# Sliding-window attention and a gated convolution block: w_in in three parts, shifted V in halves, batch 0's masks by matmul, a new order

## The chip, the cores and the metric

The kernel runs on one core of a Trainium2 chip. Its time is the device time of one execution in microseconds; the figure of comparison is the median over several executions. A profile is one execution, and has a span of its own (first to last instruction). The engines are PE (TensorE), DVE (VectorE), ACT (ScalarE), POOL (GpSimd) and SP (SyncE, which here only issues DMAs); each runs its own instructions in order and waits on semaphores for the others.

## The reference

Eight batches of 576 tokens with 8 heads of 64. The first half is attention inside a window of 32 tokens to each side; the second is a feed-forward block whose hidden layer is gated by a convolution of three taps along the sequence.

```python
scores = scale * q @ k.T                      # per batch and head
scores = where(|i - j| <= 32, scores, -1e9)
x = softmax(scores) @ v                       # -> (8, 576, 512)
h = max(x @ w_in, 0)                          # w_in (512, 1024)
conv[t] = sum_k conv_w[k] * h[t + k - 1]      # zero outside the sequence
out = (h * sigmoid(conv)) @ w_out             # w_out (1024, 512)
```

All inputs and the output are float32; the kernel computes in bfloat16 with float32 sums.

## The kernel before

**Attention.** For a batch `b` and a group `i` of four heads, `load_qk` brings q and k into a staging tile `st`, `cast_qk` turns them to bfloat16 (`qkb`), `transposes` turns them by TensorE into `qkT` (an `ev` copy of PSUM follows for each half), and `scores` makes, for 64 queries at a time, the products with the 128 keys around them. Those 128 keys are one window's reach, so that every score tile is 128 keys by 64 queries with the same band inside; `exp` (ACT) writes them to `attn`, and `mask` multiplies the result by a band of ones and zeros (DVE or POOL). No maximum is subtracted. `values` (`av`) multiplies V by it. V carries a 65th column of ones, so the sum of weights comes with the product; `rec` and `mul` divide by it.

**Plain and shifted V.** Query tiles begin every 64 tokens, so every second one needs the V rows from the middle of one 128-row block to the middle of the next. `load_v` and `cast_v` fill `ve`, with the plain blocks; `shift_v` makes `vo`, whose upper half is the lower half of `ve`'s block (`vo hi`) and whose lower half is the upper half of the next block (`vo lo`). For batches 0 and 1 this is done block by block; for the others four blocks at a time, in one operation for each half. The order says on which engine: a copy by DVE or POOL, or a DMA from SBUF to SBUF. Before, 11 of the 12 operations of batches 2 to 7 are DMAs of 260 KB, issued by SP.

**Feed-forward.** Two batches make three chunks of 384 tokens (`c` from 0 to 11); `unit` handles 128 hidden features of a chunk (`m` from 0 to 7): `ph` (four matmuls of x, turned, and `w_in`), `relu`, the three taps, `tanh`, `gate`. A tap is a matmul with a diagonal weight block (`diag_w`, built by `diag m`, three instructions), a DVE operation, or a POOL product (`cp`, and `cs` for the sum of two). The table `CONV` has a letter for each unit: 3, 2 and 1 for the number of taps on TensorE (the rest on DVE), q, r and s for kinds with POOL. Then `project` (`py`) multiplies by `w_out`, `y` copies the result and `store` writes it. `turn` brings the attention's output to x turned, by TensorE (`xt`, `ex`) or by a DMA transpose (`xd`), as `TURNS` says.

**What sets the order.** Nothing is scheduled at run time. Every operation has a number, and the string `ORDER` (lines 102 to 191) names each with its engine's letter (P, V, S, G, D for SP's DMAs) and its buffers; `Work.emit` walks it. What an engine does is thus fixed in order: what waits holds everything behind it on that engine, and for SP this means every later DMA. `F` in the order stands for filler matmuls on zeros. `load_w` brings w_in and w_out through slots of the same `st` ring in halves of 1 MB, and `cast_w` turns each 128-column block to bfloat16. Helper `InOrder` (line 232) issues every instruction, so all have that line in the profile.

POOL's order up to the last cast of batch 1's k, by names: cast v 0 0, diag 1, cast q 0 0, diag 2, 0, 5, 6, cast q 0 1, diag 7, 3, 4, two vo copies of batch 0, cast w_in 1, 0, one vo copy, cast w_in 6, 4, cast q 1 0, cast k 1 0, one vo copy, cast q 1 1, cast k 1 1.

Of the kernel before, what the change touches and what calls it, by code (L numbers as in the profile page):

```python
# [10 lines left out]
BF16 = mybir.dt.bfloat16  # L11
# [29 lines left out]
class Work:  # L41
# [44 lines left out]
BUFS = {'st': 3, 'qkb': 5, 'qkT': 3, 'attn': 2, 'rec': 4, 'xn': 3, 'hT0': 8, 'hT1': 6, 'hT2': 6, 'cp': 2, 'gT': 4, 'y': 7}  # L86
TURNS = ('eeeee', 'eeede', 'eeeed', 'dedde', 'ddddd', 'ddddd', 'ddddd', 'edddd')
CONV = (
    '33333333',
    '33q3323r23223321',  # L90
    's222r32q',
    '1232s332',
    '22q22q22',
    'q31s2qrq',
    '33212q2s',
    'r2rq312q',
    'qq23q1q2',
    'r3rqrq23',
    '12qrrq1q',
    '2rrr2rrq',  # L100
)
ORDER = """
15D 11D0 12D 1F 17D 2F 13D1 2F 14D 7F 28G 0V 1P0 2F 2V 33V 1F 4G 4F 20G0 21S 2F 16D 5G 1F 22S1 41P120 42P 23S 3G
45P34 44V 1F 43S 1F 46P 8G 2F 48S 47V 1F 9G 1F 30S 2F 49P5600 24G2 25S 54P214 2F 37V 18D 55S 1F 10G 1F 51S 1F 120D2
59P321 60P 52S 26V3 1F 27S 1F 6G 62V 1F 63P60 19D 61S 1F 64P 1F 36V 50S 121D0 1F 7G 65V 2F 130D1 66S 2F 53V 29S 1F
67P2351 1F 57S 56S 1F 35G 131D 72P604 70S 1F 31V 68S 2F 34G 1F 73S 2F 38V 74S 1F 39V 1F 58V 69S 3F 75S 123G 135D 1F
125S 77P10 86P5 124S 71V 95P2 3F 122G 78V0 96V1 1F 87V2 79S 2F 32V 132D2 2F 76V 97S 3F 40G 88V 1F 133D 98P6 89P0
113P3 99V3 107P4 90V0 104P1 100V 80P2 128G 129S 1F 114V1 105V2 1F 81V3 91V 102P5 127S 126G 106V 1F 93P6 82S 108V0
103V 139G4 109V 115S 84P7 94V 111P0 231D0 85S 112V 118P1 156P522 140G0 119V 134D 241P4 158S 157V 285P3 242S00 263P6
286S1 144V 243P7 264S2 149G 287P0 261S 150V 265P1 141G1 305S 262V 307P2 283S 306V 159P54 284V 142G2 308S3 172P360  # L110
161V 329P7 136D 174S 160V 173S 309P0 351P1 330S4 327S 331P2 232D1 352S5 328V 162P4650 233G 234S 353P3 349S 235V 137D
373P7 165S 164S 350V 163S 175P10 374V6 143G 167P526 371S 395P4 176V 236S 985D 170S 166V 375P7 169S 517P1 396S7 145G
372V 473P6 168S 177V 397P2 152G 393S 429P4 415S 171V 178P3501 138D 430S01 238S 239G 518V1 583P4 416V 181S 519P1 240S
237G 474V2 539P0 986D 394V 180S 451P2 482G0 983D2 561P6 179S 148V 495P7 481G1 584S3 188P51 151V 452S4 417P3 483G
496V5 537S 987D 189V2 190S 981D0 538V 146G 453P4 982D 183P271 182V 562S1 984D 471S 197P5 147S 418P 595G0 186S 198V3
484V6 185S 155G 199V 431P1 184S 472V 497P7 153V 421P5 419S0 154V 994V 988D 515S 187V 540S4 206P4 449S 422P 493S
992S3 450V 207V0 494V 516V 209P2 596V3 200P0 208S 191P1 218P6 996G 210V1 201V2 215P7 192V3 211V 202S 193V 542P2
219V1 213P4 216V0 423V1 195P1 217S 989D 204P0 220V 224P5 196V 990S4 425P6 991G0 225V3 543V 226V 1076D1 1017P711 214S
205V 221D 229P5 559S 426P 1077D 230S 993G1 1018V 1001P402 560V 1080D 427S2 1019V 1004P57 1078D0 627P2 1003S 1002V
1079D 605P6 1006S 715P1 997G 628V0 649P0 606S1 1005V 716S2 629P4 608P7 998G 717P2 647S 650V3 671P6 597V 735S 693P1  # L120
648V 1085G2 672S4 652P5 736V 603S 1020P04 609V 694S5 674P6 604V 625S 695P2 1022V 1021S 737P1 759P3 713S 626V 738S7
563P0 675V 760S6 793P4 714V 581S 1082D 995V 691S 1007P7130 582V 1086S3 1000D 692V 740P2 653V 764P0 815P6 741V 1008S
794V02 1010S 816V2 757S 837P7 809G1 1009S 765V 808G0 758V 1012P436 669S 838S5 766V 781P1 1087G4 670V 1014S 1015S
1081D 1013S 1096P270 1011V 779S 782P 1097S 810G 780V 1098V 1099P53 783S3 1083D 1023P6421 1016V 811P0 1100S 999D
840P7 424D 1088G0 812V 1024S 818P1 859P5 1084D 1101V 1026S 813S 420D 1025S 1112P622 1089G 841V 784D 881P3 860S4 428D
814V 1027G 1113S 1735D2 1114V 862P4 882S3 785P5 857S 819V 863V 1028P062 1737D1 1092S 1033P32 858V 1736D 835S 786P
1738D 1034V2 879S 893G1 836V 1029S 1051P7 1035V 1090G 1031S 1042P1 880V 787S4 1060P0 903P3 1091G 1052V1 1030S 1061V0
1043V3 1053V 925P2 1094D 894V4 904S1 1741D 947P5 1062V 926S0 895V 905P6 1044V 948S5 1115P73 1032V 901S 928P0 923S
955G0 1117V 789P2 1116S 1744G1 924V 1036P1 929V 1045P5 1069P3 1063P7 1054P6 1037V2 956G1 790P 1046V1 945S 1064V0
1038V 1065S 1746G2 1055V3 1047V 1070V2 1040P1 1056V 1049P5 791S5 1071V 1067P7 957G 1058P6 1050S 902V 1072D 1755P321  # L130
1068S 946V 973P4 1745G3 1059S 1756V 1041S 1740D 1102P5070 1757V 1747S4 969P6 788D 958V3 1739D 1093V 1171P1 1105S
1103S 1095D 1104S 1193P2 1172V03 967S 1106G 1215P7 1742D 1750S 1194V2 1107P501 968V 1216S1 1832D0 1176P2 1110S
1196P3 1108S 1177V 970P 1109S 1197V 1833Q 1118P7151 1743D 1178V 1749G 1213S 1237P0 1073D 1120S 1111V 1830D2 974P
1121S 1831D 1191S 1748G 1214V 1238S5 792D 1192V 1128P10 1119S 1146P5 975V6 1155P3 1137P0 971S1 1259P2 1122G 1147V1
1129V0 1156V3 1138V2 1148V 1123P746 1139S 1130V 1217P5 1260V4 1125S 1240P1 1157V 1126S 1277P0 1124S 1303P2 1241V
1835D 1235S 1274G1 1325P4 1257S 1127V 1842S0 1281P3 1275G0 1236V 1158P6 1140P7 1304V7 1326S3 1751G 1131P5 1282S6
1258V 1149P4 1752G 1164P2 1150V1 1305P3 1159V0 1165V2 1151S 1834D 1141V3 1276G 1160V 1283P1 1166V 1323S 1132V0 972D
1328P6 1142V 1754G 1301S 977P2 1278V 1302V 1279S 1144P4 1324V 1771P710 1145S 1280V 978P 1836D 1840G1 1772S 1329V
976D 1161D 1133V 1774P34 1345S 1773V 1758P07 1753D 1839G2 979S0 1347P5 1134D 1759S 1346V 980D 1776V 1844S 1841G4
1169P1 1850P262 1838D 1170S 1348P 1760V 1775S 1843G 1851V 1761P0410 1349S3 1852V 1351P7 1762S 1350D 1845G 1763S  # L140
1766P325 1764S 1853P60 1767S 1765V 1866P411 1352P 1769S 1768S 1868V 1854S 1770G 1837D 1777P3521 1867V 1353S2 1355P1
1855V 1778S 1152D 1780S 1782P647 1354D 1779S 1356P 2491D1 1785S 1784S 2492D 1783S 1781V 2489D2 1359P3 1357S4 1786V
1787P01 2490D 1360S00 1805P2 1814P5 1358D 1796P7 1806V2 1381P4 1788V1 1815V3 1807S 1797V0 1847V 1798V 1403P6 1816S
1382V1 1362P1 1846V 1384P3 1404S2 1789V 1447P7 1363V 1412G0 2495D 1385V 1425P2 1379S 1411G1 1448S3 1817P4 1380V
1401S 1413G 1790P5 1450P0 1426S4 1818V0 1791V2 1402V 1823P6 1808P7 2500G3 1428P1 1451V 1469P2 1809V3 1824V1 1467S
1429V 1810S 1799P3 1468V 1825V 1445S 1491P0 1800V3 1414V7 1826D 1470S5 2501S2 1547P6 1446V 1477G0 1801V 1513P2
2498G1 1492V0 1423S 1869P13 1792V 1548S21 1424V 1494P0 1514S1 1793D 1478G1 1569P5 1870V 1871S 2494D 1479G 2499S4
1827D 1516P6 1819V 1535P7 1495V 1820D 1555G1 1517V 1570S4 1591P2 1511S 1480V3 1533S 1613P1 1512V 1556G0 1489S 2493D
1534V 1592S1 1571P4 1802D 2504G 1614V3 1848D 1635P5 1589S 1557G 1490V 1849D 1596P0 1856P6210 1590V 1636S0 1536P
1597V 1628G0 1857S 1558V3 1859S 1858S 2496D 1861P456 2503G 1598V 1567S 1631P1 1811D 1539P2 1862S 1860V 1611S 1629G1  # L150
1568V 1701P4 1864S 1863S 1612V 1630G 1540P 1537S5 1702V5 2502S 1538D 1872P6351 1865V 1541S1 1877P074 2497D 1874S
1709G1 1632V 1657P2 2584D0 1879S 1710G0 1542D 1679P3 1878S 2586D1 1711G 1875S 1882P72 1873S 2587D 1891P0 1900P5
1883V1 1880S 1892V3 1633S 1909P6 1884V 1638P4 1658S4 1881V 1543P7 2585Q 2505G 1893V 1680S2 1910V2 1925P2 1634V 1911S
1665G0 2589D 1901V0 1639V 2507D 1544P 1926S22 1902V 1655S 1876V 1927P0 1545S6 1947P3 1712V1 2506S 1546D 1656V 1918P6
1945S 1691G1 1894P2 1885P5 1948S0 1919V1 1903P7 1946V 1912P4 1721S 1991P3 1895V3 1913V2 1904V0 1896S 1920V 2508D
2593G0 1914V 2035P0 1886V1 1905S 1722V 2509P640 1887V 1921D 1969P2 1992S1 1692V1 2510S 2594G1 2511V 1949P5 1970S5
2013P7 1693V 2036S6 1888D 1666G1 1967S 1727P3 2014V7 1699S 1667G 1968V 2016P6 1700V 2079P4 1922D 2592Q 2043G1 2017V
# [36 lines left out]
def kernel(  # L194
# [67 lines left out]
    diag_w = sb.tile([128, 3, MB, 128], BF16, name="diag_w")  # L262
    ident = sb.tile([128, 128], BF16, name="ident")
    ident24 = sb.tile([3 * MB, 3 * MB], FP32, name="ident24")
    mask = sb.tile([128, 18, 64], BF16, name="mask")
    zero = sb.tile([128, 512], BF16, name="zero")


# [541 lines left out]
```

The softmax here doesn't subtract the row's maximum and nothing guards it: scores larger than these inputs give would overflow.

## Time and profile before

| | us |
|---|---|
| median of 13 executions (lowest, highest) | 228.05 (225.87, 230.52) |
| the profiled execution: time, span | 230.52, 228.8 |
| first feed-forward matmul (`pf<-xT,w_in_sb`) | 25.48 |
| busy: PE, DVE, ACT, POOL | 212.1, 197.7, 187.4, 140.0 |
| half clock granted in the attention and feed-forward work, near | 90 to 94 |
| DMA moved in all | 48.16 MB |

A line of a group or a time line names the engine, the operation, the tile written and those read, with shapes, and in brackets the idle time before it and what ended it. The clock row has a digit for each fortieth of the span (5.72 us), in tenths of full speed, and 9 is full. Matmuls overlap, so the mean duration of one is longer than the time from start to start.

### The profile page before, as it was taken

The page shows a single profiled execution, that of the slowest core. Times are in us where ns is not written, and L with a number is a line of the kernel's source. Part 1 is how long each engine was busy: PE and PEld are TensorE (multiplying, and loading weights), DVE is VectorE, ACT ScalarE, POOL GpSimd, SP SyncE. Part 2 cuts the span into 40 slices and gives each one's busy share as a digit, 9 for nine tenths or more (in the row PEclk, how much of TensorE's full clock was granted, in tenths as well). Part 3 has the DMA queues.
Part 4 walks back from the last instruction along what each step waited for, and adds up shares of the span by engine and source line. Part 5 has one row for each costly group of instructions (what it writes and reads, how often), then busy time and mean ns, then how long its engine had stood idle before and what let it go on. Part 6 is the DMA issues. An engine that isn't in the chain of part 4 may idle for free.

```text
span 228.8 us, 7189 instructions
## 1 busy us (share of the span) xinstructions
PE 212.1 (93%) x2720; PEld 123.1 (54%) x2720; DVE 197.7 (86%) x467; ACT 187.4 (82%) x474; POOL 140.0 (61%) x203
## 2 busy tenths in 40 slices
PE   7698899989989995999999988999999999999993
PEld 5367558558455642555555545545555565455441
DVE  6289779899999985698899868998999999899990
ACT  2699899998989694789989979779979899777642
POOL 5988656653575855784268945865475745476540
PEclk9799999999999998899999999999999999999999
DMA  6999999999989999999994999995606311501224
GB/s 194 342 290 376 360 263 252 340 295 287 256 227 328 246 144 293 315 241 201 279 314 99 185 263 370 180 204 155 186 14 133 105 46 37 183 1 49 92 93 182
DMA packets 66390, 48.16 MB, mean 211 GB/s; under 512 B 50780, under 2 KB 50804, under 8 KB 66356
## 3 DMA queue, kind: packets, MB, share of 16 engines
q1 hardware_dynamic: 64992, 46.32, 77.2%
q10 hardware_dynamic: 1364, 1.39, 3.4%
q8 instruction: 21, 0.34, 0.8%
q14 instruction: 13, 0.11, 0.2%
HBM read 32.52 MB, written 9.44 MB: 183 GB/s over the span
## 4 chain that ended last, share of the span: by engine, by line
PE 52%; ACT 14%; DMA 13%; DVE 13%; issue 4%; POOL 2%; SPq 1%; DVEq 0%; POOLq 0%; ACTq 0%
PE pf L232 52%; DMA vst<-in_v_dram 10%; ACT attn L232 5%; DVE gT L232 3%; DMA st<-in_k_dram 3%; DVE pf L232 3%; DVE qkT L232 2%; ACT pf L232 2%; ACT xn L232 1%; ACT qkb L232 1%; DVE attn L232 1%; DVE xn L232 1%; ACT y L232 1%; DVE hT L232 1%; DMA xT<-xn 1%
## 5 line engine op out<-in xcount | busy, mean ns | idle before, releaser
L232 PE MATMUL pf<-xT,w_in_sb 128*128 128x385 bf16 (+2 forms) x416 | 74.0, 317 | 3.2 <-ACT hT L232 0.7
L232 PE MATMUL pf<-w_out_sb,gT 128*128 128x512 bf16 x288 | 72.2, 380 | 0.0
L232 POOL TENSOR_SCALAR cp<-hT,conv_w_sb 128x384 f32<-128x384 bf16 (+1 forms) x63 | 40.3, 645 | 47.5 <-ACT hT L232 20.0
L232 ACT ACTIVATE pf<-pf 128x384 f32<-128x384 f32 (+1 forms) x104 | 48.4, 479 | 12.3 <-DVE pf L232 10.2
L232 DVE SCALAR_TENSOR_TENSOR gT<-pf,hT 128x384 bf16<-128x384 f32 (+1 forms) x104 | 52.1, 517 | 5.4 <-ACT pf L232 4.9
L232 PEld LDWEIGHTS <-w_in_sb 128*128 128x128 bf16 x416 | 38.8, 98 | 27.2 <-issue 3.6
L232 ACT ACTIVATE attn<-pf 128x512 bf16<-128x512 f32 (+1 forms) x96 | 41.4, 523 | 2.4 <-PE pf L232 2.4
L232 ACT ACTIVATE hT<-pf 128x385 bf16<-128x385 f32 (+2 forms) x76 | 35.6, 490 | 6.0 <-PE pf L232 5.7
L232 PEld LDWEIGHTS <-gT 128*128 128x128 bf16 x288 | 26.0, 98 | 25.8 <-DVE gT L232 0.5
L232 DVE SCALAR_TENSOR_TENSOR pf<-hT,conv_w_sb,pf 128x384 f32<-128x384 bf16 (+1 forms) x61 | 34.7, 586 | 2.0 <-PE pf L232 1.9
L232 PE MATMUL pf<-hT,diag_w 128*128 128x384 bf16 (+1 forms) x153 | 31.5, 313 | 0.9 <-DVE xn L232 0.6
L232 POOL TENSOR_SCALAR qkb<-st 128x1152 bf16<-128x1152 f32 (+1 forms) x23 | 25.9, 1124 | 8.5 <-DMA st<-in_k_dram 3.9
L232 DVE COPY qkT<-pf 128x576 bf16<-128x576 bf16 x35 | 25.6, 749 | 4.6 <-PE pf L232 4.6
L232 ACT ACTIVATE xn<-pf,rec 128x64 bf16<-128x64 f32 x96 | 21.9, 355 | 5.5 <-DVE rec L232 5.4
L232 POOL TENSOR_TENSOR cp<-cp,cp 128x384 f32<-128x384 f32 (+1 forms) x24 | 24.5, 1022 | 1.6
L232 DVE TENSOR_TENSOR attn<-attn,mask 128x1152 bf16<-128x1152 bf16 x26 | 22.9, 880 | 2.2 <-ACT attn L232 2.1
L232 DVE SCALAR_TENSOR_TENSOR pf<-hT,conv_w_sb,cp 128x384 f32<-128x384 bf16 (+1 forms) x35 | 21.4, 624 | 0.0
L232 ACT COPY y<-pf 128x512 f32<-128x512 f32 x30 | 18.1, 607 | 3.6 <-PE pf L232 3.4
L232 POOL TENSOR_TENSOR attn<-attn,mask 128x1152 bf16<-128x1152 bf16 x6 | 14.2, 2372 | 9.2 <-ACT attn L232 9.2
L232 ACT COPY qkT<-pf 128x576 bf16<-128x576 bf16 x29 | 18.6, 666 | 0.7 <-PE pf L232 0.5
L232 PEld LDWEIGHTS <-diag_w 128*128 128x128 bf16 x153 | 13.5, 99 | 10.4 <-issue 2.1
L232 DVE TENSOR_TENSOR xn<-pf,rec 128x256 bf16<-128x256 f32 x48 | 18.9, 409 | 0.0
(49 smaller groups left out, 235.4 us busy)
## 6 DMA issues: line engine op xcount, KB each, us to landing
st<-in_q_dram SPq DMA_DIRECT2D x16, 576.0 KB, 6.8
out_dram<-y SPq DMA_DIRECT2D x36, 256.0 KB, 3.4
st<-in_k_dram SPq DMA_DIRECT2D x14, 576.0 KB, 7.5
vst<-in_v_dram SPq DMA_DIRECT2D x24, 256.0 KB, 7.0
vst<-in_v_dram SPq DMA_DIRECT2D x15, 192.0 KB, 5.3
vo<-ve SPq DMA_DIRECT2D x11, 260.0 KB, 5.8
st<-in_moe_w_in_dram SPq DMA_DIRECT2D x2, 1024.0 KB, 9.4
st<-in_moe_w_out_dram SPq DMA_DIRECT2D x2, 1024.0 KB, 9.6
```

Source lines behind the costliest of these rows:

```text
L232: return lambda *args, **kwargs: fixed(do(*args, **kwargs))
```

## The change

It has these parts.

- **Loads.** w_in comes in three DMAs (blocks 0 and 1, 2 and 3, 4 to 7); SP's first loads are q, k and q of batch 0, then V.
- **Shifted V.** Batches 2 to 7 make it in two halves of two blocks: 24 operations, of which 11 are by POOL, 5 by DVE and 8 by DMA. Over all batches 18 are on POOL, 13 on DVE and 9 are DMAs.
- **Masks of batch 0.** A kind `a` of scores first adds -30000 outside of the band: three matmuls into each group of three PSUM banks (`outside`, a 64 by 128 block for each half of partitions, times the identity), and then accumulates the scores on them. No `mask` follows. The table `MASKS` chooses it for batch 0 only.
- **Buffers.** `BUFS` has four `st` tiles for three, six `qkb` for five, seven `rec` for four, and other counts of xn, hT, gT and y.
- **Order.** `ORDER`, `CONV` and one entry of `TURNS` are new. There are 37 filler matmuls for 75, 132 full-width and 34 half-width taps on TensorE for 118 and 35, 14 turns by TensorE for 16, and 32 of the transposing DMAs for 29. In DVE's and ACT's order, qkT copies are 23 and 41 for 35 and 29.

POOL's order up to the last cast of batch 1's k is now: cast q 0 0, cast k 0 1 (two parts), diag 1, cast v 0 1, diag 0, cast v 0 2, cast v 0 3, one vo copy of batch 0, cast v 0 4, cast w_in 0, 2, 1, diag 2, cast w_in 5, cast q 1 0, cast w_in 7, diag 6, 4, 3, 5, 7, cast q 1 1, two `cp` and a `cs` of chunk 0's unit 5, cast w_out 1, vo lo 1 0, cast v 1 2, vo lo 1 1, cast k 1 1.

```diff
-BUFS = {'st': 3, 'qkb': 5, 'qkT': 3, 'attn': 2, 'rec': 4, 'xn': 3, 'hT0': 8, 'hT1': 6, 'hT2': 6, 'cp': 2, 'gT': 4, 'y': 7}
+BUFS = {'st': 4, 'qkb': 6, 'qkT': 3, 'attn': 2, 'rec': 7, 'xn': 2, 'hT0': 6, 'hT1': 7, 'hT2': 9, 'cp': 2, 'gT': 3, 'y': 5}
+MASKS = ('aa', 'mm', 'mm', 'mm', 'mm', 'mm', 'mm', 'mm')
...
+    gpsimd.memset(outside, 0.0)
+    for half in range(2):
+        rows = slice(64 * half, 64 * half + 64)
+        gpsimd.affine_select(
+            out=outside[rows, :], in_=outside[rows, :], compare_op=ALU.is_ge, fill=-30000.0, base=0,
+            pattern=[[1, 128]], channel_multiplier=-1,
+        )
...
+    W_PARTS = {"in": ((0, 2), (2, 4), (4, MB)), "out": ((0, MB // 2), (MB // 2, MB))}
+    first_load = {}
+
     def load_w(which, i):
-        s = w_slot[which, i] = Slot(ring)
+        m0, m1 = W_PARTS[which][i]
+        n, at = m1 - m0, d_model * (m0 % 4)
+        s = w_slot.setdefault((which, m0 // 4), Slot(ring))
...
-            def emit(e_, x=x, ps=ps, todo=todo):
-                for x_, e, t in todo:
-                    n = col(x_, e, t) - 1152 * x
+            def emit(e_, x=x, ps=ps, todo=todo, added=False):
+                if added:
+                    for n, e, width in ((2, x, 2), (0, 0, 8), (1, 1, 8)):
+                        rows = slice(64 * e, 64 * e + 64)
+                        tensor.matmul(
+                            ps[n].ap[:, 0:64 * width].rearrange("p (t x) -> p t x", x=64), outside[rows, :],
+                            ident[rows, None, rows].broadcast_to([64, width, 64]), start=True, stop=False,
+                        )
...
-        for c in range(NBLK - 1) if b < 2 else (0,):
-            shift_v(b, c, c + 1 if b < 2 else NBLK - 1)
+        for c in range(0, NBLK - 1, 1 if b < 2 else 2):
+            shift_v(b, c, c + (1 if b < 2 else 2))
...
-            for i in range(2):
+            for i in range(len(W_PARTS["in"])):
                 load_w("in", i)
...
+    kinds.update({("mask", b, i): MASKS[b][i] for b in range(B) for i in range(2)})
```

## The prediction

> **What bounds the kernel now.** I read the page's busy shares and clock row first, then busy time by stretch, then who waited for whom, and last the engines' own time lines at the places these named.
>
> ```profile
> PE 212.1 (93%) x2720; PEld 123.1 (54%) x2720; DVE 197.7 (86%) x467; ACT 187.4 (82%) x474; POOL 140.0 (61%) x203
> ...
> PEclk9799999999999998899999999999999999999999
> DMA  6999999999989999999994999995606311501224
> ```
>
> TensorE is busy 93% of the span, so what counts is when its real work starts, how much there is, and what it waits for in between. DMA is full until about 145 us.
>
> ```profile
> 0.00:25.48 25.48, 20.43 (x329) 14.05 (x330) 17.81 (x56) 18.54 (x46) 19.79 (x65) 0.93 1.00 303
> 25.48:35.00 9.52, 9.52 (x137) 5.79 (x137) 6.51 (x14) 8.35 (x19) 5.74 (x8) 1.00 1.09 314
> 35.00:60.60 25.60, 24.63 (x377) 17.52 (x375) 24.51 (x68) 24.61 (x73) 12.40 (x17) 1.00 1.15 290
> 60.60:101.80 41.20, 37.14 (x552) 20.78 (x547) 35.51 (x83) 32.61 (x79) 28.99 (x28) 0.96 1.05 256
> ```
>
> The columns are the stretch, its length, busy us of PE, weight load, DVE, ACT and POOL, the granted clock, the DMA share and GB/s. The first feed-forward matmul starts at 25.48 us. In the 9.5 us after it TensorE never rests, while POOL works 5.7 of them: POOL has cleared its desk. From 60.6 to 101.8 TensorE idles 4.1 us, and its clock drops.
>
> ```profile
> 5.29 1.17 POOL L232 TENSOR_SCALAR diag_w<-ident,conv_w_sb 128x128 bf16<-128x128 bf16 x3 [1.03 <-DVE conv_w_sb L232]
> 7.03 4.21 POOL L232 TENSOR_SCALAR diag_w<-ident,conv_w_sb 128x128 bf16<-128x128 bf16 x12
> 11.81 3.52 POOL L232 TENSOR_SCALAR diag_w<-ident,conv_w_sb 128x128 bf16<-128x128 bf16 x9
> ...
> 18.14 2.15 POOL L232 TENSOR_SCALAR w_in_sb<-st 128x512 bf16<-128x512 f32 x2 [0.43 <-DMA st<-in_moe_w_in_dram]
> ...
> 21.80 1.20 POOL L232 TENSOR_SCALAR w_in_sb<-st 128x512 bf16<-128x512 f32 x2
> 23.17 1.15 POOL L232 TENSOR_SCALAR qkb<-st 128x1152 bf16<-128x1152 f32 x1 [0.17 <-DMA st<-in_q_dram]
> ...
> 29.16 1.16 POOL L232 TENSOR_SCALAR qkb<-st 128x1152 bf16<-128x1152 f32 x1 [0.32 <-PE pf L232]
> ```
>
> All 24 diagonal weight blocks (8 operations of 3) are built by 15.3 us, while POOL would otherwise wait for loads. The last cast of batch 1's k is done at 30.3 us, before TensorE can use it.
>
> ```profile
> 86.88 0.22 PE L232 MATMUL pf<-ve,attn 128*64 128x65 bf16 x1
> 89.92 0.19 PE L232 MATMUL pf<-vo,attn 128*64 128x65 bf16 x1 [2.82 <-DMA vst<-in_v_dram]
> ```
>
> This is the largest single wait. The first multiplication by the plain V goes, the one by the shifted V three microseconds later: what is late is the shifted V of batch 3, issued by SP at 83.20 (behind a store whose issue took 3.5 us), not the V load that the profile names. The clock row then shows 8 for two slices: the array runs at half rate for some 3.4 us, which costs 1.7 more.
>
> **What the Trainium skill says.** "TensorE: Matmul & The Clock Gate", part 1, has a free-running activity window of about 3.4 us that sets full or half clock. The trace agrees: one window with TensorE busy 17% (86.9 to 90.4 us) and one with 41% (5.0 to 8.4) are followed by half clock, windows of 69% and more are not. "DMA: Bandwidth & Descriptors", anatomy of one DMA, says that a wait is done by the issuing sequencer, not by the DMA engines; so a shifted-V transfer that waits for its casts holds all later loads on SP. The trace's 5.8 us from issue to landing of the vo transfers is what such a copy costs in a full queue. "GPSIMD Engine Reference", side-by-side cycle accounting, has 1.03 cycles an element at 1.2 GHz for such one-input work: 0.89 us for the new 1040-element copy, before dispatch. The trace has 0.69 us for 520 and 1.92 for 2080 elements; on that line 1040 takes 1.10, which I use.
>
> **The change part by part.** *Lead-in.* SP now issues q, k, q, then V; w_in goes in 0.5, 0.5 and 1 MB. The first k is behind one transfer instead of two, and the V block before it was 192 KB: 0.6 us at the 303 GB/s of the first row. The fifth V block is behind 0.5 MB less: 1.7 us. The first exponential follows the four copies of qkT; without the two pairs of fillers ahead of the first scores, and with k earlier, I put it 1.2 us earlier than 12.27. The four masks of batch 0 (0.88 us each, two of them in the last 2.2 us before the first multiplications of the second half) are replaced by 12 matmuls, 8 of 512 and 4 of 128 columns: 8 x 0.217 + 4 x 0.06 = 2.0 us of TensorE, hidden, since TensorE waits for ACT there and 38 fillers go (75 take 12.8 us, so 6.5). So the gain is between 1.2 us (ACT decides) and 3 us (V and masks decide). I take 2.1: first feed-forward matmul at 23.4.
>
> *More matmul work.* Taps on TensorE by the new table: full width 11 + 17 x 2 + 29 x 3 = 132 against 118, half width 34 against 35. At 0.165 us (start to start, as in four 385-column matmuls in 0.83 us, of which the last takes 0.33) that is 14 x 0.165 - 0.08 = 2.2. Two turns less by TensorE give 0.45 back; batch 1's first q transposes move behind the start, 0.37. Sum +2.1. Counts of the other engines fall: DVE about 8 us (12 qkT copies, 13 taps and 3 masks fewer, 4 more other sums), ACT about 4. About half of DVE's is lead-in; the rest hides behind TensorE.
>
> *POOL.* The order puts only three diagonal operations ahead of the w_in casts' end; five come after them, 5 x 1.06 = 5.3 us, and the casts of batch 1's q and k are queued behind. From the moment POOL reaches w_in block 5: that cast 0.6, q cast 1.15, block 7 0.6, five diagonals 5.3, second q cast 1.15, two taps 1.28 and their sum 1.04 (chunk 0 now has one such unit), a w_out cast 0.62, two vo copies 1.32, a V cast 0.65, k cast 1.16: 14.9 us. It reaches block 5 at 22.3: the last V block lands near 18, its cast takes 0.65, three w_in casts 2.4 (between 0.6 and 1.07 each above), one diagonal 1.06. The q load is next in the queue after the last w_in part and lands near 23.7, 0.8 later than POOL is ready. So the k cast ends at 22.3 + 14.9 + 0.8 = 38.0. TensorE stands ready for it after 8 w_in blocks (32 x 0.166 = 5.3), 19 taps (3.1), 12 half-width matmuls (1.0), three transposes (1.1), two scores (0.8): 11.4 us after 23.4, and with 0.6 of small waits at 35.4. It waits 2.6 us, and everything of TensorE is behind it. From below: 0.8 us if POOL runs its diagonals at their best rate (0.35 each) and the casts at 0.6; from above 4. Two thirds of a clock window idle can bring half clock: between 0 and 1.7, I take 0.7.
>
> *Shifted V.* Eleven transfers of 260 KB leave SP's queue; eight halves and one block remain, 18 copies go to POOL and 13 to DVE. The queue loses over half of those bytes (11 x 260 against about 9 x 130 KB). The stall at 86.9 should go, since batch 3's shifted V is asked for ten us of matmul work ahead: -3.0 - 1.7 in the profiled run. POOL's added copies, about 11 us over the span, lie beside 61% busy. New waits come: one half of batch 5 is issued only some 2.2 us of matmul work ahead of its use against 5.8 us to land in a full queue; batch 2's last half is copied just before its use; one mask of batch 7 sits on POOL (2.37 us) in front of its use. 0 to 4, I take 0.8, since the same places also wait now.
>
> *Sum against the profiled execution:* its span is 228.8 and its time 230.52, the slowest of 13; the median is 2.5 lower. A stall with a clock drop is just what varies between executions, so I count half of the 4.7 us for the median. Median: 228.05 - 2.1 + 2.1 + 2.6 + 0.7 - 2.35 + 0.8 = 229.8. Against the profiled run with all of the 4.7 it would be 230.52 - 0.6 = 229.9. I say 229.7.
>
> **The rivals.** *The queue's relief pays for all (faster).* The place is 60 to 145 us, where DMA is full and TensorE idles 6.3 us of 85; if loads and shifted V come in time, 3.5 of these go, and if POOL's backlog costs only 0.8 without a clock drop, the time is 228.05 - 2.1 + 2.1 + 0.8 - 3.5 = 225.3. It decides from where POOL's k cast is done within 1 us of TensorE's arrival. For it: DMA at 1.05 and the drop at 86.9; against it: POOL's queue as counted.
>
> *They cancel (same).* Backlog 1.6, relief 2.0: 228.05 - 2.1 + 2.1 + 1.6 - 2.0 + 0.4 = 228.05. For it: all terms are of one size.
>
> *POOL becomes the bound more widely (clearly slower).* POOL has 12.4 us of 25.6 busy from 35.0 to 60.6 now and gets some 7 more before 60 us. If its order also makes V and w_out late there, and the clock drops twice: 2 more for waits, 1.5 for the clock, 233.2. Against it: 19 of 25 us still fit.
>
> That the shifted V doesn't leave the queue is only true for nine of 40 copies.
>
> **How the numbers follow.** The likeliest, POOL's backlog with most of the relief, 0.38 at 229.7 (its own range 228.2 to 231.5); wide POOL bound 0.15; cancel 0.2; relief 0.27. A difference below 0.5% (1.14 us) cannot be told from none by these runs. Faster than 226.9: 0.27. Between 226.9 and 229.2: 0.2, the cancelling case (its upper tail and the likeliest one's lower edge, each over 229.2 and under it, are about even). Slower: 0.53. The range must reach into both signs: 225.2 to 233.5.
>
> **What would show it.** Right: the first matmul of xT and w_in at 22.5 to 24.3 us; a TensorE wait of 2 to 4 us before transposes near 35 to 39, ended by a qkb cast on POOL; diagonal builds on POOL after 24 us; no wait of 3 us on vo near 87; DVE near 190 busy. Wrong: no POOL wait before 40 us, or the chain passing through DVE or ACT instead; a first matmul later than 25; idle of TensorE between 60 and 145 us as large as now.

## The result and the profile after

| | us |
|---|---|
| changed kernel, median of 11 executions (lowest, highest) | 231.48 (229.22, 234.03) |
| kernel before, measured beside it, median | 227.76 |
| ratio, 95% interval | 1.0163 (1.0129 to 1.0198) |
| profiled execution of the changed kernel: time, span | 232.73, 231.0 |
| first feed-forward matmul | 24.81 |

The change makes the kernel 1.6% slower, 3.7 us. The medians here and below are of all executions, while a ratio and its interval leave out those more than 1.5% above the fastest of their kernel, so a ratio can differ by some tenths of a per cent from that of the two medians. The busy shares, the clock row and the DMA row of the changed kernel, and the shifted V's rows among its groups and DMA issues, are these.

```profile
PE 211.0 (91%) x2701; PEld 122.8 (53%) x2701; DVE 194.3 (84%) x454; ACT 184.1 (80%) x460; POOL 148.1 (64%) x222
...
PEclk9955999999999999999999999999999999999999
DMA  6999999986999967999999699952332334312053
...
L233 POOL TENSOR_SCALAR vo<-ve 64x1040 bf16<-64x1040 bf16 (+1 forms) x18 | 17.0, 949 | 5.2 <-ACT ve L233 4.1
...
vo<-ve SPq DMA_DIRECT2D x8, 130.0 KB, 3.5
```

Every engine but POOL has less busy time than before, and the span is longer: the time went into waiting. POOL has 8 us more. The queue is relieved as planned (eight transfers of 130 KB, 3.5 us from issue to landing, where 260 KB took 5.8), and half clock is granted for 10.2 us of the lead-in, where it was 3.4 before, and no longer near 90 us. By stretch (length; then busy us of PE, weight load, DVE, ACT and POOL; clock; DMA share; GB/s):

```profile
0.00:24.81 24.81, 18.88 (x284) 12.78 (x285) 14.46 (x52) 15.75 (x38) 14.29 (x58) 0.79 1.01 293
24.81:60.60 35.79, 32.35 (x495) 21.80 (x495) 29.81 (x70) 30.38 (x79) 28.88 (x48) 1.00 0.98 273
60.60:101.80 41.20, 40.68 (x643) 23.44 (x641) 38.11 (x89) 39.26 (x100) 32.89 (x35) 1.00 0.95 254
101.80:145.60 43.80, 38.27 (x515) 21.59 (x508) 34.77 (x86) 34.17 (x84) 27.40 (x28) 1.00 1.03 236
```

The second row has 28.9 us of POOL in 35.8; before, the 35.1 us from the first feed-forward matmul to 60.6 had 18.1 (5.74 and 12.40, the two rows shown there). TensorE rests 3.4 us of it, where it rested 1.0 before. From 60.6 to 101.8 the 4.1 us of rest are down to 0.5. From 101.8 to 145.6 it rests 5.5; before it rested 2.3, as this row of the kernel before shows:

```profile
101.80:145.60 43.80, 41.54 (x572) 23.06 (x571) 38.26 (x90) 38.77 (x102) 27.10 (x31) 1.00 0.98 244
```

So from 60.6 to 145.6 the rest only changed its place: 6.1 us in all, for 6.3 before. POOL's time line from its second q cast of batch 1 to the last k cast, then the stretch of TensorE's that waits for that cast:

```profile
26.32 5.28 POOL L233 TENSOR_SCALAR diag_w<-ident,conv_w_sb 128x128 bf16<-128x128 bf16 x15
31.56 1.15 POOL L233 TENSOR_SCALAR qkb<-st 128x1152 bf16<-128x1152 f32 x1
32.69 1.15 POOL L233 TENSOR_SCALAR cp<-hT,conv_w_sb 128x384 f32<-128x384 bf16 x2
...
37.71 1.32 POOL L233 TENSOR_SCALAR qkb<-st 128x1152 bf16<-128x1152 f32 x1
```

```profile
39.09 0.43 PE L233 MATMUL pf<-ident,qkb 64*128 64x64 bf16 x18 [1.38 <-POOL qkb L233]
40.69 0.45 PE L233 MATMUL pf<-qkT 64*128 64x64 bf16 x18 [0.56 <-ACT hT L233]
```

The five diagonal builds take 5.28 us, the k cast ends at 39.03, and TensorE has waited 1.4 us for it; another 0.56 follow before the scores. The later loss has one large item, in TensorE's time line and in SP's:

```profile
132.32 0.22 PE L233 MATMUL pf<-vo,attn 128*64 128x65 bf16 x1 [2.40 <-DMA vo<-ve]
```

```profile
126.59 0.59 SPq L233 DMA_DIRECT2D vo<-ve  x1
...
127.92 1.29 SPq L233 DMA_TRANSPOSE xT<-xn  x1
129.31 0.54 SPq L233 DMA_DIRECT2D vo<-ve  x1
```

That is `vo lo 5 0 2`, one of the four pieces of batch 5's shifted V. It is issued at 129.3, behind other pieces, loads and transposing DMAs, and the values of batch 5 need it at 129.7.

To compare whole stretches over kernels, I gave each TensorE operation the time from its start to the next start that operations of its kind typically have in the kernel before; what is left of a stretch is waiting. This estimate from single executions splits TensorE's time as follows. The second row is the kernel of the last experiment below.

| profiled execution | first feed-forward matmul | waits to 60 us | 60 to 100 | 100 to 145 | 145 to 190 | matmul work |
|---|---|---|---|---|---|---|
| before | 25.5 | 3.1 | 8.1 | 4.5 | 1.2 | 181.8 |
| before, one transfer earlier | 25.8 | 2.8 | 4.7 | 4.7 | 1.1 | 181.8 |
| changed | 24.8 | 5.8 | 2.4 | 7.5 | 1.9 | 184.3 |

After 145 us TensorE hardly waits in any of them. Against the second row, whose order differs from the kernel before by one transfer, the changed kernel's TensorE ends 5.3 us later (226.8 for 221.5): start -1.0, waits +3.0, -2.3, +2.8, +0.8 and -0.5 (190 us to the end), work +2.5. Executions of one kernel lie up to 4 us from its median, so this shows the places; the sizes are the medians' affair.

### The profile page after: what moved, and what is told of

Same layout as the page of the kernel before. It is cut to its first block, busy times and chain, and to the rows that moved or that the text cites. A ratio compares the mean times of both kernels' runs of the same rounds, so it can differ in the third digit from the quotient of the medians.

```text
span 231.0 us, 7121 instructions
## 1 busy us (share of the span) xinstructions
PE 211.0 (91%) x2701; PEld 122.8 (53%) x2701; DVE 194.3 (84%) x454; ACT 184.1 (80%) x460; POOL 148.1 (64%) x222
## 4 chain that ended last, share of the span: by engine, by line
PE 59%; ACT 10%; DMA 9%; DVE 9%; SPq 5%; issue 4%; POOL 3%; POOLq 0%; ACTq 0%; DVEq 0%
PE pf L233 59%; SPq L233 5%; DMA vst<-in_v_dram 4%; DMA st<-in_q_dram 3%; DVE pf L233 3%; DMA st<-in_k_dram 3%; ACT attn L233 2%; ACT pf L233 2%; ACT qkT L233 2%; DVE gT L233 2%; ACT hT L233 2%; DVE attn L233 1%; POOL qkb L233 1%; DVE xn L233 1%; POOL cp L233 1%
## 5 line engine op out<-in xcount | busy, mean ns | idle before, releaser
L233 PE MATMUL pf<-hT,diag_w 128*128 128x384 bf16 (+1 forms) x166 | 34.1, 310 | 2.6 <-ACT hT L233 1.5
L233 POOL TENSOR_SCALAR qkb<-st 128x1152 bf16<-128x1152 f32 (+2 forms) x24 | 26.8, 1122 | 11.0 <-DMA st<-in_k_dram 7.8
L233 DVE SCALAR_TENSOR_TENSOR pf<-hT,conv_w_sb,pf 128x384 f32<-128x384 bf16 (+1 forms) x50 | 29.1, 594 | 1.6 <-PE pf L233 0.6
L233 ACT COPY qkT<-pf 128x576 bf16<-128x576 bf16 x41 | 25.3, 653 | 3.4 <-PE pf L233 3.4
L233 POOL TENSOR_SCALAR ve<-vst 128x512 bf16<-128x512 f32 x23 | 15.9, 698 | 10.7 <-DMA vst<-in_v_dram 9.6
L233 POOL TENSOR_TENSOR cp<-cp,cp 128x384 f32<-128x384 f32 (+1 forms) x22 | 21.4, 975 | 1.8
L233 ACT ACTIVATE xn<-pf,rec 128x64 bf16<-128x64 f32 x80 | 18.6, 331 | 2.6 <-DVE rec L233 2.3
L233 POOL TENSOR_SCALAR vo<-ve 64x1040 bf16<-64x1040 bf16 (+1 forms) x18 | 17.0, 949 | 5.2 <-ACT ve L233 4.1
L233 DVE TENSOR_TENSOR attn<-attn,mask 128x1152 bf16<-128x1152 bf16 x23 | 20.0, 869 | 0.4 <-ACT attn L233 0.4
L233 ACT COPY y<-pf 128x512 f32<-128x512 f32 x26 | 15.5, 609 | 5.8 <-PE pf L233 5.8
```

The lines of the kernel that those rows point to most:

```text
L233: return lambda *args, **kwargs: fixed(do(*args, **kwargs))
```

## The experiments

The theories were: (A) POOL's queue before the k cast is the cause of the early loss; (B) a few late DMAs from 100 to 145 us; (C) the half clock of the lead-in; (D) the added matmul work; and against all of these, (E) that no one place is the cause: each wait that is repaired is taken over by the next engine in the new order. Each ratio is to executions of the kernel before that were measured beside it. Diffs of the order name the operations; `ORDER` has numbers for them.

### Diagonal blocks built early

```diff
-consts, conv_w, conv_ev (what the blocks are built from) where they were
+consts, conv_w, conv_ev ahead of DVE's first cast q 0 1
-POOL: cast k 0 1, diag 1, cast v 0 1, diag 0, ... diag 2, cast w_in 5, cast q 1 0, cast w_in 7, diag 6, 4, 3, 5, 7, cast q 1 1
+POOL: diag 1, 0, 2, 6, 4, cast k 0 1, diag 5, cast v 0 1, diag 3, cast v 0 2, ... diag 7, cast w_in 5, cast q 1 0, cast w_in 7, cast q 1 1
```

> The changed kernel, with the diagonal weight blocks built where POOL waits for the first k (five of eight before that cast, one each before two V casts and before w_in's block 5), and their source, the conversion of conv_w, made early. POOL's backlog as the cause: the cast of batch 1's second k ends at 34 to 36 us instead of 39.0, TensorE's wait before its transposes (1.5 us) and the 1.8 us of small waits around it go, and the time falls by 2 to 3 us, to about 229. Extra tap work as the cause: no more than 0.7 us falls, since the wait moves to the next late thing (w_out or V). Half clock in the lead-in as the cause: no change.

Measured: 231.68 us against 228.85, ratio 1.0116 (1.0054 to 1.0179). The five builds are gone from POOL's backlog, and the k cast still ends at 38.3. POOL's time line of this kernel shows where the 5.3 us went.

```profile
28.67 1.15 POOL L231 TENSOR_SCALAR qkb<-st 128x1152 bf16<-128x1152 f32 x1 [2.32 <-DMA st<-in_q_dram]
...
32.16 1.16 POOL L231 TENSOR_SCALAR cp<-hT,conv_w_sb 128x384 f32<-128x384 bf16 x2 [2.33 <-DVE hT L231]
```

POOL now idles 2.32 us for the q load and 2.33 for the hidden features of unit 5, which stand ahead of the k cast in its order. So the backlog was one of three things that the cast had to wait for, and they ended at nearly the same time.

### The k cast ahead of the rest of the queue

```diff
 POOL (with the early diagonal blocks): ... cast q 1 1, two cp and cs of unit 5,
-cast w_out 1, vo lo 1 0, cast v 1 2, vo lo 1 1, cast k 1 1
+cast k 1 1, cast w_out 1, vo lo 1 0, cast v 1 2, vo lo 1 1
```

> The diagonal blocks early as in the run before, and the cast of batch 1's second k moved on POOL ahead of one w_out cast, two vo copies and a V cast (behind the tap products of chunk 0's unit 5, which kept it late when the diagonals no longer did). POOL's queue as the cause, of which the diagonals were only the first part: the cast ends by 36, TensorE's waits at the transposes and the scores after them (2.3 us in the changed kernel) go, ratio to the kernel before about 1.005. If this stretch is set by ACT and DVE anyway: the waits move to scores or taps before 45 us and the ratio stays at 1.01.

Measured: 232.17 us against 228.24, ratio 1.0217 (1.0148 to 1.0287). The cast ends at 36.8 and no transpose waits for POOL any more. TensorE's time line of this kernel:

```profile
37.65 0.65 PE L231 MATMUL pf<-hT,diag_w 128*128 128x384 bf16 x3 [0.45 <-ACT attn L231]
41.59 0.46 PE L231 MATMUL pf<-qkT 64*128 64x64 bf16 x18 [1.10 <-DVE qkT L231]
```

The wait is back one step later, at the scores, for DVE's copy of the transposed k. The waits to 60 us are 5.6 us by the accounting, for 5.8. This takes POOL's queue out as the cause of the early loss: with its wait gone, the waits are there. How the ratio of this run came to be the highest of the repairs isn't shown; its profiled execution has 17.1 us of half clock in the lead-in (10.1 to 27.2) for the changed kernel's 10.2, and its first feed-forward matmul is at 25.85.

### The transposes of that k moved ahead as well

```diff
 TensorE (with the two edits above):
-ph 1 2 and what follows it, tr k 1 1
+tr k 1 1, ph 1 2 and what follows it
 the copies of tr k 1 1: ahead of an exp on ACT, of a mask on DVE
```

> The kernel with the early diagonals and the early k cast, and the transposes of that k moved ahead in TensorE's order by two blocks of chunk 1 (their two copies of PSUM moved ahead of an exponential on ACT and of a mask on DVE). If TensorE's own fixed order keeps the wait after POOL was repaired (it moved from the transposes to the scores that need their copies, 1.27 us): that wait falls under 0.5 us, and TensorE reaches chunk 0's projection 1 us or more earlier, counted from the first feed-forward matmul, than in the run with the early cast (16.5 us there, 16.6 in the changed kernel, 15.4 for 1.4 us more of work in the kernel before). The ratio to the kernel before is then 1.01 or less. If ACT and DVE set this stretch, the wait moves again and the ratio stays at 1.015 to 1.02.

Measured: 232.02 us against 228.45, ratio 1.0144 (1.0087 to 1.0202). In this kernel's time line of TensorE one wait has become three, ended by ACT and DVE:

```profile
38.31 0.42 PE L231 MATMUL pf<-ident,qkb 64*128 64x64 bf16 x17 [0.53 <-DVE hT L231]
40.21 0.33 PE L231 MATMUL pf<-hT,diag_w 128*128 128x192 bf16 x2 [0.70 <-ACT hT L231]
41.30 0.45 PE L231 MATMUL pf<-qkT 64*128 64x64 bf16 x18 [0.42 <-ACT hT L231]
```

The waits to 60 us are still 5.8 us, and the first projection of chunk 0 starts 16.6 us after the first feed-forward matmul, as in the changed kernel; in the four profiles with the order of before it is 15.3.

### A late piece of batch 5's shifted V issued earlier

```diff
 SP:
-load v 6 2, ..., xd, vo hi 5, load, xd, vo lo 5 0 2
+load v 6 2, vo lo 5 0 2, ..., xd, vo hi 5, load, xd
```

> The changed kernel, with one half of batch 5's shifted V issued by SP some 20 us earlier, right after a V load. If its late issue (129.3 us, in the profile) is a true cost, TensorE's wait of 2.6 us at 129.7 goes, and 1.5 to 2.6 us of time. If other late work stands behind it (the relu at 138.8, DMAs of the turns), less than 0.7 us.

Measured: 230.85 us against 228.85, ratio 1.0101 (1.0027 to 1.0175). The 2.4 us wait at 132 is gone, and what TensorE waits for between 100 and 145 us falls from 7.5 to 3.2. The ratio is 0.6% (1.4 us) under that of the changed kernel, less than the wait that went, and the intervals overlap. The kernel is still slower than before.

### Filler matmuls in the lead-in

```diff
 TensorE's order up to the first feed-forward matmul: 32 more F (37 -> 69 in all)
```

> The changed kernel with 32 filler matmuls added at TensorE's waits of the lead-in, where the granted clock is half from 11.8 to 22.0 us. Half clock as a cause: full clock from about 12 us, first feed-forward matmul 0.5 to 1 us before 24.8, and as much off the time. If ACT and the V loads set the lead-in: the clock is full, the first feed-forward matmul within 0.3 us of 24.8 and the time within 0.5 us of 231.5; fillers in front of ready work may cost some tenths.

Measured: 231.26 us against 228.85, ratio 1.0119 (1.0085 to 1.0154). The clock row of this kernel:

```profile
PEclk9999999999999999999999999999999999999998
```

In this execution the half clock is gone up to the last slice, where TensorE has nothing left to do, and the first feed-forward matmul is at 24.7 for 24.8. The fillers cost something too: the first exponential starts at 11.03 us for 10.30. Over all executions the half clock is less but not gone: the mean granted clock is 0.975 to 1.0 (median 0.990), for 0.961 to 0.985 (0.970) in the changed kernel. The ratio is 0.4% (1 us) below that of the changed kernel, and the intervals overlap. Taken together they leave room for anything from no cost to some 2 us (an estimate from the two intervals).

### The three repairs together

```diff
+ the early diagonal blocks, the k cast ahead, vo lo 5 0 2 early, 32 F
```

> All repairs of the changed kernel together: diagonals and the k cast early on POOL, batch 5's shifted V issued early, fillers in the lead-in. If each cause is its own: -2.3 for POOL, -2 for batch 5, -0.5 for the clock, ratio about 0.995. If the kernel is held by something that all of them leave (the balance of DVE, ACT and TensorE after 60 us): 1.005 to 1.01.

Measured: 230.74 us against 228.24, ratio 1.0151 (1.0089 to 1.0213). The gains don't add to the 0.995 of the first case. By the medians alone it is 1.011, so between hardly anything and a third of the loss is recovered. The places moved again, as TensorE's waits between 100 and 145 us in this kernel show (total, times, longest):

```profile
PE pf L232 <- ACT hT L232: 2.1, 1, 2.1
PE pf L232 <- DMA xT<-xn: 1.6, 1, 1.6
```

### Two taps for three on TensorE, and the reverse in the kernel before

```diff
 changed kernel, 14 units of chunks 2, 3, 4, 7 and 11, e.g. chunk 2:
-'s333333s'
+'s222222s'
```

> The changed kernel with 14 full-width units of chunks 2, 3, 4, 7 and 11 moved from three taps on TensorE to two, the middle one by DVE: as many taps on TensorE as before the change. The extra matmul work as the cause: 14 x 0.165 = 2.3 us off the time, about 229.2. If DVE has no room (14 x 0.6 = 8.4 us more): nothing is gained, or 1 to 3 us lost, with more ACT waits on DVE.

```diff
 kernel before, 14 units of chunks 2, 3, 4, 7, 9, 10 and 11, e.g. chunk 2:
-'s222r32q'
+'s333r33q'
```

> The kernel before with 14 full-width units of chunks 2, 3, 4, 7, 9, 10 and 11 moved from two taps on TensorE to three: as many taps on TensorE as the changed kernel. If TensorE's work sets the time: 2.3 us more, ratio 1.01. If DVE sets it as much (8.4 us fewer there): between 0.99 and 1.0, and more matmul work is no loss by itself.

Measured: in the changed kernel 235.99 us against 228.85, ratio 1.0316 (1.0256 to 1.0376); in the kernel before 228.06 against 228.45, ratio 0.9984 (0.9957 to 1.001). Fourteen taps taken back from TensorE cost 1.5%, with DVE busy 200.9 us for 194.3 and TensorE waits more in the middle of the span, where the largest such item of the changed kernel is 0.7 (60 to 125 us; total, times, longest):

```profile
PE pf L231 <- ACT hT L231: 1.7, 2, 0.9
PE pf L231 <- DVE gT L231: 1.6, 2, 0.9
...
```

The same edit the other way round, 2.3 us more matmul work, costs the kernel before nothing that can be measured; VectorE's busy time falls there from 197.7 to 192.5 us. What is priced is thus the trade of VectorE's work for TensorE's, which is the one that the change makes. (D) falls: the added work isn't where the loss is.

### Masks of batch 0

```diff
 changed kernel:
-MASKS = ('aa', 'mm', 'mm', 'mm', 'mm', 'mm', 'mm', 'mm')
+MASKS = ('mm', 'mm', 'mm', 'mm', 'mm', 'mm', 'mm', 'mm')
 and four masks on DVE
```

> The changed kernel with batch 0's masks by DVE again, each right after the exponentials of its half (the scores without the 12 matmuls). If the masks by matmul shorten the lead-in: first feed-forward matmul 1 to 2 us after 24.8, ratio 1.02 or more. If DVE has room there: first matmul within 0.5 us, ratio within 0.5% of 1.016.

```diff
 kernel before:
+    added = b == 0    # 12 matmuls of `outside` into the scores' banks
-    mask 0 0, mask 0 1 on DVE (four operations)
```

> The kernel before with one part of the change alone: batch 0's band masks by 12 matmuls of TensorE on a block that GpSimd builds, the four mask operations of VectorE in the lead-in taken out, everything else and its order as before. VectorE is busy for 9.94 of the 10.5 us from 15.0 to 25.5 us in the kernel before, and its four masks of 0.88 us each lie there. If the masks on VectorE are on the lead-in's path: the first feed-forward matmul comes 0.5 to 1.5 us before the 25.5 us of the kernel before, and the ratio is 0.993 to 0.997. If the landing of V's last block, which VectorE casts at 19.95 us, sets the lead-in: the first feed-forward matmul within 0.3 us of 25.5, and the ratio within 0.3% of 1.

Measured: without the new masks the changed kernel takes 234.85 us against 228.45, ratio 1.0259 (1.0203 to 1.0316), and its first feed-forward matmul comes at 27.4 us. The clock row of this kernel has more half clock than that of the changed one, from 11.1 to 28.2 and from 134.0 to 140.8 us:

```profile
PEclk9955599999999999999999959999999999999999
```

The edit takes 12 matmuls from TensorE as well as giving VectorE four masks, so how much of the later start is the masks and how much the clock isn't shown.

In the kernel before, the new masks alone give 227.59 us against 228.17, ratio 0.9953 (0.9917 to 0.9988): the only interval here that ends below 1, and just so. The medians alone differ by 0.25%, so this is at the edge of what can be told. Where the masks pay there stays open. The ratio is where the theory of VectorE's masks had it, but in the profile the first feed-forward matmul is at 25.60, not earlier. The profiled execution took 229.96 us, more than the kernel's median. The stretch from 15 to 25.5 us, before and with the new masks:

```profile
15.00:25.50 10.50, 8.95 (x178) 6.42 (x176) 9.94 (x27) 10.25 (x33) 7.54 (x10) 1.00 1.09 350
```

```profile
15.00:25.50 10.50, 9.28 (x186) 6.90 (x183) 6.89 (x23) 10.37 (x32) 6.70 (x12) 1.00 1.09 352
```

VectorE loses 3.05 us of work (its four masks took about 0.75 us each here, less than the 0.88 of the expectation, which is their mean over the kernel), and ScalarE is busy without a pause in both, 10.25 and 10.37 us of 10.5. That fits ScalarE holding the lead-in in the order of before, so that VectorE's masks alone don't shorten it.

### The added copies back to DMAs

```diff
 changed kernel, 11 halves of batches 2 to 7:
-vo lo / vo hi on POOL
+vo lo / vo hi by DMA, issued by SP at the same place of the order
```

> The changed kernel with the 11 halves of shifted V of batches 2 to 7 that POOL copies issued as DMAs by SP at the same places of the order. The relief of the DMA queue as a gain of the change: undone, it costs 2 to 4 us (waits of SP for the V casts hold later loads; vo waits on TensorE as at 87 us in the kernel before), ratio 1.025 or more. POOL's copies as a loss of the change: POOL is 12 us freer, and the ratio falls below 1.01. Neither matters: within 0.5% of 1.016.

Measured: 238.4 us against 228.24, ratio 1.0422 (1.0322 to 1.0523). TensorE's time line has a wait of 5.7 us of a kind that the changed kernel has nowhere between 60 and 100 us:

```profile
76.46 0.26 PE L231 MATMUL pf<-vo,attn 128*64 128x65 bf16 x1 [5.67 <-DMA vo<-ve]
```

In this order the copies by POOL are worth 2.6%. The edit keeps each place in the order, which was laid out for copies, so it measures the copies in this order and not in any other.

### The 87 us stall of the kernel before

```diff
 kernel before, SP:
-store 1 1, load v 4 0, vo lo 3 0 4
+vo lo 3 0 4, store 1 1, load v 4 0
```

> The kernel before with one edit: SP issues the late half of batch 3's shifted V ahead of one store and one V load, so about 2.4 us earlier. If the wait of 3 us at 86.9 and the half clock after it are a cost in most executions: ratio to the kernel before 0.985 to 0.99 (2.4 to 3.5 us). If other waits there are as late: 0.995 to 1.0.

Measured: 228.09 us against 228.24, ratio 1.0036 (1.0006 to 1.0066). The clock row of the page, and the stretch in which the stall was:

```profile
PEclk9889999999999999999999999999999999999999
```

```profile
60.60:98.00 37.40, 35.80 (x551) 20.32 (x545) 35.61 (x83) 32.28 (x79) 27.52 (x26) 1.00 1.08 269
```

No stall of 3 us and no half clock near 90 us, a profiled span of 225.4 for 228.8 us: and the median is no better. That fits most executions of the kernel before not having this stall; that another one takes its place isn't excluded. The granted clock speaks for the first: two stretches of half clock as in the profiled execution are 6.8 us, and in 18 of the 26 executions of the kernel before that were measured here the mean clock is 0.989 or more, which leaves some 5 us at most. The profile with the new masks in the kernel before has a stall of its own, elsewhere. Its time lines of SP, ScalarE and TensorE:

```profile
132.97 4.97 SPq L232 DMA_DIRECT2D vo<-ve  x1
```

```profile
136.07 0.62 ACT L232 CAST ve<-vst 128x512 bf16<-128x512 f32 x1 [1.67 <-DMA vst<-in_v_dram]
```

```profile
137.53 2.73 PE L232 MATMUL pf<-xT,w_in_sb 128*128 128x385 bf16 x8 [1.91 <-ACT hT L232]
```

TensorE waits for a relu that stands on ScalarE behind a cast of V, and this cast waited 1.67 us for its load. The last V load that SP had issued left at 132.12, before its long issue, so that issue isn't shown to be the reason. This execution has half clock from 137.5 to 141.0. So two profiled executions of nearly the same order have a stall at two places; what decides the place isn't shown.

## Why the prediction was right, and where it was not

The direction was right, and 231.5 us lies in the range, at the upper edge of the likeliest case's own (228.2 to 231.5). It lies as near to the 233.2 of the wider POOL bound as to the 229.7 that was named: a loss of 1.65 us was forecast and 3.7 came. Part of the agreement is luck. POOL's backlog, the step that decided for slower, is there but isn't what costs the time, and the errors of the other steps partly cancel.

Of the signs that were listed, the late diagonal builds, the wait for POOL before the transposes (1.4 us, not 2 to 4) and the absence of the 3 us wait near 87 came. The start (24.81 for 22.5 to 24.3) and VectorE's busy time (194.3 for near 190) missed. One sign of being wrong came as well: TensorE's idle time between 60 and 145 us is as large as before (6.1 us for 6.3).

**The lead-in**, -2.1: right in direction, mis-sized. The first feed-forward matmul is at 24.81 for the predicted 23.4 and the 25.48 of before: -0.7. In four profiles whose lead-in is the changed kernel's, apart from fillers in one, it came at 24.3 to 24.7, so -0.7 to -1.2. The first exponential came even earlier than worked out (10.30 us, 2.0 before that of the old kernel, for 1.2), but from there to the first feed-forward matmul it takes 14.5 us where it took 13.2. The step left that stretch as it was or shorter, and let the masks or V decide up to 3 us. Without its new masks this order starts at 27.4, so they are worth 2.6 us *in this order*, the clock included; in the order of before, the masks alone bring no earlier start. The new masks mostly pay for what the new order of the lead-in costs.

**More matmul work**, +2.1: the size was right (184.3 against 181.8 us by the accounting, +2.5), its price wrong. The same amount in the kernel before costs nothing measurable (0.9984), and taking it back from the changed kernel costs 1.5%. The step added TensorE's work to the time because TensorE is busy 93%. It left out that a tap by TensorE comes off DVE, and the run with the taps taken back shows TensorE waiting for `gT` and `hT` when it goes back. A share of 93% busy was read as if every added microsecond must lengthen the span. The 8 us counted off VectorE were 3.4: copies, taps and masks went as counted, but new work came that the sum left out, such as ten copies of `y` for six and four casts of q and k for one.

**POOL's backlog**, +2.6: right in place, about half to three quarters in size as a wait, wrong as a cause. Predicted: k cast done at 38.0, TensorE waits 2.6 us near 35.4. Measured: 39.0, and 1.4 plus 0.56 us, ending at 39.1 and 40.7. Diagonal builds stand on POOL from 26.3 to 31.6, as listed under what would show it. But freeing POOL of 5.3 us of builds moved the cast by only 0.7 us, and getting the cast out of the way (36.8) moved the wait to DVE's copy. The early loss of about 3 us is spread over POOL, DVE and ACT.

**Half clock**, +0.7: wrong in place, its price open. The step put it after the wait for POOL. There the window has TensorE busy 51%, and full clock follows. The changed kernel has 10.2 us of half clock in the lead-in (11.8 to 22.0), after a window of 65%, and none later while TensorE works. The two windows (length, busy us of PE, clock in the window, DMA share, GB/s):

```profile
8.38:11.79 3.41, 2.21 (x68) 1.00 1.20 277
35.69:39.10 3.41, 1.74 (x17) 1.00 1.13 248
```

So the limit that the prediction read from the kernel before, between 41% and 69%, isn't one, since half clock followed 65% and not 51%: the busy share of a window doesn't decide by itself. "TensorE: Matmul & The Clock Gate" in the Trainium skill, part 1, explains half clock by idle windows. These traces agree in part: 32 more fillers remove it in the profiled execution, but the window ahead of it isn't idle. Its price lies between nothing and some 2 us by the intervals, so the 0.7 can be neither confirmed nor excluded; the first feed-forward matmul moved by 0.1 us.

**Relief of the queue**, -2.35: the wrong step that mattered most for the range's lower end. As a statement on the profile it was right: no 3 us stall near 87, and rest of 0.5 us for 4.1 from 60.6 to 101.8. As a term of the median it was not seen: it counted half of a stall that the kernel before has in its profiled execution, and issuing one transfer earlier takes that stall away without a gain. Against that kernel's profile the changed one saves 2.3 us of waits between 60 and 100 us (4.7 to 2.4), and this was all that the rival of the queue's relief could draw on. The prediction had itself noted that the profiled run was the slowest of 13.

**New waits**, +0.8: the place was right, the size too small. Batch 5's half was named; it costs 2.4 us of waiting, issuing it earlier takes about 0.6% off the ratio, within the noise, and the whole stretch from 100 to 145 us waits 2.8 us more than in the second row of the table. The named mask of batch 7 and half of batch 2 didn't show as waits of that size.

**What stays open.** Two parts of the change were shown to be no cause: the masks and the copies for shifted V each make the changed kernel faster than it is without them. A third, the matmul work, costs nothing measurable where it is put into the kernel before. The half clock can be at most part of the loss. The two places where TensorE waits more can be repaired, one by one or together, with ratios from 1.0101 to 1.0217 whose intervals all overlap that of the changed kernel: the best of them, batch 5's piece issued early, recovers 0.6 of 1.6% by its ratio. All but the run with fillers have only six executions and an interval of 0.6 to 0.7% either way, some 1.5 us, so a cost of 1 us at one place can't be told from none. This fits (E): the loss lies in how the new order couples DVE, ACT and POOL to TensorE as a whole. That is argued from what was excluded and not shown by a run. The three parts of w_in and the new buffer counts weren't tried apart from the order.

## What to carry to other kernels

In a kernel whose order is written out and in which four engines are 64 to 91% busy, a wait in the profile names the operation that came last and not the cause: before pricing its removal, look up what would have come last without it, on every engine that feeds the same step. Before a stall is counted as a gain, ask if the median has it: where the profiled execution is the slowest of 13, much of what it shows to be repaired isn't there in the others. And work moved to the busiest engine isn't a cost by itself if it comes off the engine that this one waits for.

## What was not expected of the hardware

- Ten microseconds at half clock in a stretch where TensorE waits for others had no cost that can be told from none: ratio 1.0119 with most of them gone, 1.0163 with them, the intervals overlapping, and the start of the real work at 24.7 and 24.8 us.
- Half clock followed a window in which TensorE was busy 65% and not a later one of 51% in the same execution.
- One issue of a shifted-V DMA of 260 KB on SP took 4.97 us in one execution of the old order, and SP's next store left at 138.03. The size doesn't explain it: in the changed kernel such issues took 0.47 to 4.19 us with pieces of at most 130 KB (4.19 for one of batch 3), and in the kernel before 0.47 to 3.00 with 260 KB.
- POOL's copies of 1040 elements took 1.13 us on average (1.05 at best), between the 0.69 for 520 and 1.92 for 2080 of the kernel before: near the 1.10 that was read off that line.
